# Sketched attention feeding a rational MLP on one core: the same steps in another order, some of them on other engines

## The chip, the cores and the metric

One core of a Trainium2 chip. The metric is the device time of the whole program in microseconds (us), lower is better (a run more than 1.5% above the fastest of its kernel counts as slow). The profile is one execution of the program; its **span** runs from the first to the last instruction and is 1.7 to 1.8 us shorter than the time of that same execution. Engines: PE multiplies matrices, DVE and ACT work on 128 partitions of elements, POOL (GpSimd) here issues DMAs, SP issues loads and stores.

## The reference, cut to what matters

```python
# attention with a polynomial sketch, 4 batches x 4 heads x 1088 tokens x 32
a, b = S1 @ x, S2 @ x                        # 8 features each
phi = outer(a, b)                            # 64 features, for q and for k
kv, z = phi(k)^T v, sum(phi(k))
attn = (phi(q) kv) / (phi(q) z + 1e-6)
# then, on 4352 tokens of 128 channels, with 2048 hidden columns
h = attn @ w_in
P = a0 + a1*h + a2*h*h + a3*h*h*h
Q = 1 + |b0|*|h| + |b1|*h*h
out = (P / (Q + 1e-6)) @ w_out
```

## The kernel before

The kernel is a list of 589 steps. Each step names what it needs and which buffers it takes and gives back. Two constants decide the program: `ENGINE` says on which engine a step runs that may run on several, and `ORDER` says in which order all steps are issued. An engine executes its own steps strictly in that order.

```python
BUFS = dict(xT=3, hb=4, s=2, u=4, t=4, ..., h_ps=3, out_ps=1, w_ps=1, ..., oT=1)
ENGINE = {"k00.ea": "DVE", "k01.ea": "DVE", ..., "g1.ts": "DVE", ..., "g17.us": "DVE", "g18.ts": "DVE", "o8.eT": "DVE"}
ORDER = [27, 4, 26, 30, 0, 36, 1, 31, 6, ...]        # 589 numbers

def issue(self, order):                              # of the plan
    for i in order:
        s = self.steps[i]
        assert all(a["n"] in done for a in s["after"]), s["name"]
        for key in s["take"]:
            self.slot[key] = free[key[0]].pop(0)
        s["fn"]()
        ...
```

Most of the time goes to 20 groups (g0 to g19) of hidden columns, mostly 4096 elements per partition. One group is these steps:

```python
# g.e*  PSUM (where PE leaves its results) -> bf16 copies of h            ACT, or DVE where ENGINE says so
# g.ab  u = |hb|      g.sq  s = hb*hb       DVE
# g.hi  t = a3*hb+a2  g.cu  t = t*s         DVE
# g.lo  hb = a1*hb+a0                       DVE
def add(dst, src, name):                    # g.us: u += s    g.ts: t += hb
    if ENGINE.get(name) == "DVE":
        nc.vector.tensor_add(out=d, in0=d, in1=s)
    else:                                   # an accumulating DMA, issued by GpSimd
        nc.gpsimd.dma_start(out=d, in_=s, accum_op=AX.add, max_dma_last_dim=4096)
# g.ln  L = Ln(u*lsc + 1)   g.ex  u = Exp(-L)        ACT   (1/Q)
# g.ov  t = t*u             DVE    then g.pj: t @ w_out on PE
```

`kBC.*` are steps for keys, `qN.*` for queries, `oN.eT` and `oN.st` the copy and store of an output chunk, `ld.*` loads, `fN` matmuls without use, meant to keep PE's clock up (`SKIP` names those that are left out).

Of the kernel before, what the change touches and what calls it, by code (L numbers as in the profile page):

```python
# [27 lines left out]
ENGINE = {  # L28
    "ld.S0": "ACT", "ld.S1": "ACT", "ld.a": "ACT", "ld.b": "ACT", "k00.ea": "DVE", "k01.ea": "DVE", "kr.ev": "DVE",
    "kr.ea": "DVE", "k0.s0": "DVE", "q1.ev": "DVE", "q2.ev": "DVE", "k20.ea": "DVE", "q5.xe": "DVE", "k30.ea": "DVE",  # L30
    "k31.ea": "DVE", "q7.ev": "DVE", "q8.xe": "DVE", "g1.ts": "DVE", "o0.eT": "DVE", "o1.eT": "DVE", "g7.e4": "DVE",
    "o3.eT": "DVE", "o5.eT": "DVE", "g13.e4": "DVE", "g17.us": "DVE", "g18.ts": "DVE", "o8.eT": "DVE",
}

FOUR = []
SKIP = ["f3"]

HOME = {
    "k00.T": "h_ps", "k00.ab": "h_ps", "k01.T": "h_ps", "k01.ab": "h_ps", "kv.0": "h_ps", "q0.T": "h_ps",
    "q0.xT": "h_ps", "q1.T": "h_ps", "k11.T": "h_ps", "q2.T": "h_ps", "q2.xT": "h_ps", "q3.T": "h_ps",  # L40
    "q3.xT": "h_ps", "k20.T": "h_ps", "k21.T": "h_ps", "kv.2": "h_ps", "q4.T": "h_ps", "q5.T": "h_ps",
    "q6.T": "h_ps", "q8.T": "h_ps", "q8.xT": "h_ps", "fill.1": "h_ps", "fill.4": "h_ps", "fill.6": "h_ps",
    "fill.9": "h_ps", "fill.11": "h_ps", "fill.12": "h_ps",
# [3 lines left out]
    27, 4, 26, 30, 0, 36, 1, 31, 6, 56, 20, 3, 32, 33, 37, 5, 41, 38, 39, 57, 23, 46, 29, 2, 42, 40, 58, 43, 47, 59,  # L47
    60, 44, 45, 48, 49, 50, 51, 52, 21, 53, 28, 55, 8, 61, 7, 83, 78, 79, 67, 54, 62, 63, 80, 81, 11, 34, 68, 69, 12,
    64, 65, 84, 22, 9, 66, 82, 70, 71, 72, 85, 86, 215, 216, 35, 217, 10, 87, 218, 230, 232, 231, 233, 24, 245, 16,
    220, 219, 115, 247, 116, 246, 248, 222, 224, 234, 235, 237, 223, 221, 226, 73, 74, 75, 249, 250, 238, 239, 240,  # L50
    76, 25, 251, 93, 94, 236, 77, 252, 253, 254, 227, 266, 268, 270, 88, 89, 267, 269, 256, 257, 241, 242, 95, 97,
    272, 271, 225, 14, 228, 273, 229, 243, 104, 105, 90, 258, 244, 96, 91, 92, 274, 277, 285, 98, 130, 201, 117, 99,
    100, 255, 260, 286, 13, 275, 131, 279, 259, 287, 101, 278, 289, 291, 261, 262, 288, 118, 119, 276, 200, 290, 292,
    102, 103, 120, 121, 263, 293, 294, 296, 297, 281, 306, 106, 307, 108, 122, 123, 325, 326, 280, 107, 109, 124,
    264, 298, 282, 283, 308, 309, 310, 312, 152, 295, 311, 313, 300, 265, 110, 111, 112, 327, 284, 153, 329, 314,
    315, 331, 328, 317, 318, 319, 330, 132, 332, 205, 125, 126, 301, 113, 213, 154, 334, 18, 114, 299, 155, 134, 302,
    333, 127, 128, 129, 316, 133, 346, 303, 336, 135, 338, 17, 156, 348, 321, 337, 304, 347, 349, 189, 350, 320, 190,
    365, 203, 157, 351, 322, 323, 352, 15, 136, 366, 141, 158, 137, 353, 138, 142, 335, 340, 305, 324, 367, 368, 355,
    354, 139, 339, 357, 358, 359, 369, 140, 386, 159, 341, 371, 370, 372, 342, 160, 376, 373, 374, 377, 378, 387, 19,
    143, 145, 356, 361, 360, 343, 388, 389, 344, 161, 390, 392, 391, 393, 144, 167, 362, 168, 146, 405, 395, 375,  # L60
    406, 162, 163, 164, 165, 345, 380, 381, 166, 363, 409, 147, 397, 394, 148, 149, 364, 398, 399, 407, 411, 408,
    379, 382, 150, 151, 410, 412, 414, 416, 413, 418, 169, 171, 396, 383, 178, 401, 426, 427, 428, 429, 170, 417,
    172, 179, 384, 445, 402, 430, 431, 432, 173, 446, 174, 181, 400, 433, 403, 175, 435, 404, 434, 415, 420, 437,
    180, 182, 176, 447, 177, 448, 419, 451, 421, 183, 438, 439, 449, 422, 450, 452, 454, 453, 385, 466, 467, 209,
    436, 441, 468, 469, 423, 485, 486, 424, 456, 457, 184, 185, 186, 440, 442, 470, 471, 458, 487, 472, 204, 488,
    489, 473, 443, 474, 475, 444, 477, 478, 455, 460, 191, 193, 425, 459, 187, 188, 479, 491, 490, 492, 192, 461,
    493, 194, 462, 506, 525, 526, 508, 507, 476, 494, 480, 195, 196, 463, 527, 496, 497, 464, 481, 509, 482, 498,
    495, 510, 511, 512, 513, 528, 465, 529, 483, 197, 514, 198, 515, 517, 519, 499, 500, 484, 530, 531, 214, 532,
    501, 548, 546, 533, 207, 534, 547, 516, 535, 502, 549, 553, 518, 536, 538, 520, 561, 562, 563, 537, 564, 551,
    550, 552, 521, 522, 523, 574, 540, 503, 504, 575, 576, 554, 577, 539, 555, 541, 208, 542, 566, 524, 579, 581,  # L70
    580, 568, 567, 569, 557, 558, 565, 570, 571, 505, 199, 578, 556, 559, 582, 543, 211, 206, 212, 544, 545, 210,
    560, 572, 573, 583, 584, 585, 586, 587, 588, 202,
# [40 lines left out]
def kernel(  # L113
# [243 lines left out]
    W_by = [big.tile([128, NF // 2, d_model], BF, name=f"w_by{i}") for i in range(4)] if FOUR else []  # L357
    by_steps = []
    if FOUR:
        ld["wf"] = load("wf", lambda key: starter(key).dma_start(  # L360
            out=new("L", "wf")[:, :NF // 2 * d_model].rearrange("p (n d) -> p n d", d=d_model),
            in_=moe_w_out.rearrange("(fo fi) d -> fi fo d", fi=128)[:, 0:NF // 2, :]), 1740, pk=1024, take=[("L", "wf")], start="SP")

        def by(i):
            o, s = W_by[i].rearrange("p n d -> p (n d)"), T["L", "wf"][:, :NF // 2 * d_model]
            if ENGINE.get(f"c.w{i}", "ACT") == "ACT":
                nc.scalar.mul(o, s, a_sb[:, i:i + 1])
            else:
                nc.vector.tensor_scalar(out=o, in0=s, scalar1=a_sb[:, i:i + 1], scalar2=None, op0=AX.mult)

        for i in range(4):
            alts = dict(ACT=280 + 0.82 * NF // 2 * d_model, DVE=150 + 0.55 * NF // 2 * d_model)
            by_steps.append(plan.add(f"c.w{i}", ENGINE.get(f"c.w{i}", "ACT"), alts[ENGINE.get(f"c.w{i}", "ACT")], lambda i=i: by(i),
                                     after=[ld["wf"], c_inv], give=[("L", "wf")], alts=alts))

# [39 lines left out]
    def add_keys(b):  # L415
# [44 lines left out]
        s = plan.add(f"k{b}.rem", "PE", 540, accumulate_rem, after=[prev, krem_step[0], ld["vr"]])  # L460
# [19 lines left out]
    def add_queries(n, srcs, nt, owners, loads, kv_steps, give=()):  # L480
# [41 lines left out]
        def divide():  # L522
            nb = min(2, nt)
            nd = pair("nd")[:, :nt // nb, :nb * 132].rearrange("p b (g c) -> p b g c", c=D + 1)
            den = new("den", n)[:, :nt // nb, :nb * H]
            nc.vector.tensor_scalar(out=den, in0=nd[:, :, :, D], scalar1=1e-6, scalar2=None, op0=AX.add)
            nc.vector.reciprocal(out=den, in_=den)
            x = new("x", n)[:, :nt, :].rearrange("p (b i) (h d) -> p b (i h) d", b=nt // nb, h=H)
            nc.vector.tensor_mul(out=x, in0=nd[:, :, :, 0:D],
                                 in1=den[:, :, :, None].broadcast_to([128, nt // nb, nb * H, D]))  # L530

        def x_transposes():
            p = new(*ps(nm, "xT"))
            for i in range(nt):
                nc.tensor.transpose(p[:, i * 128:(i + 1) * 128], in_=T["x", n][:, i, :], identity=ident)

        def x_evac():
            o, i = new("xT", n)[:, :W], T[ps(nm, "xT")][:, :W]
            if ENGINE.get(nm + ".xe", "ACT") == "ACT":
                nc.scalar.mul(o, i, sig)  # L540
            else:
                nc.vector.tensor_scalar(out=o, in0=i, scalar1=sig, scalar2=None, op0=AX.mult)
# [3 lines left out]
        ex = [plan.add(f"{nm}.ex{i}", "PE", 900 * W // 512 + 80, lambda i=i: expand(i), after=[s, c_rep],  # L546
# [5 lines left out]
        for i in range(nt // 2):  # L552
            nd.append(plan.add(f"{nm}.nd{i}", "PE", 520, lambda i=i: num_den(i), after=[s] + nd + kv_steps,
                               take=[("h_ps", nm, "nd")] if i == 0 else [], give=[("q_pT", n)]))
        s = plan.add(f"{nm}.dv", "DVE", 560 + 135 * nt, divide, after=nd, take=[("x", n), ("den", n)],
                     give=[("h_ps", nm, "nd"), ("den", n)])
        s = plan.add(nm + ".xt", "PE", 100 * nt + 37, x_transposes, after=[s], take=[ps(nm, "xT")], flex=[ps(nm, "xT")], give=[("x", n)])
        return add_copy(nm + ".xe", x_evac, W, ptr=1, after=[s, c_b], take=[("xT", n)], give=[ps(nm, "xT")])


# [224 lines left out]
```

## Time and profile before

| | before |
|---|---|
| time, median of the first 3 runs | 251.48 us (251.42 to 254.35, and that last one counts as slow) |
| profiled execution | 250.56 us, span 248.8 |
| DVE busy / ACT busy | 225.4 / 213.7 us |
| DMA: queue 0, that is the accumulating sums and w_out | 79.7% of the span |

Busy time is time in which at least one instruction of the engine runs. How these lines are read, and those of the waits and timelines, stands in the prediction, which shows them.

The timelines of DVE and POOL before (start, duration in us) have:

```profile
28.11 1.79 DVE L585 TENSOR_SCALAR u<-hb 128x2048 int16<-128x2048 int16 x1
...
26.83 1.34 POOL L594 DMA_DIRECT2D u<-s  x1 [23.34 <-DVE u L585]
27.51 1.88 POOL L265 DMA_DIRECT2D w_out<-in_moe_w_out_dram  x1
```

The same mask takes 0.69 us elsewhere. Here it runs while GpSimd issues two DMAs one upon the other.

### The profile page before, as it was taken

The numbers are of one execution on the slowest core, as the hardware profiler recorded it, in microseconds if no ns is written. First come the engines' busy times: TensorE is split into PE (matmuls) and PEld (weight loads), VectorE is DVE, ScalarE is ACT, GpSimd is POOL, SyncE is SP. The second block draws the span as 40 slices with busy tenths as digits, with TensorE's granted clock in tenths as the row PEclk, the third lists the DMA queues.
The fourth block names the chain that finished last, engine by engine and source line by source line (L and its number), as shares of the span: only waits on it lengthen the run. The fifth ranks groups of instructions, "written<-read, shape, count | busy, mean of one in ns | idle before, by whom it ended". The sixth has DMA issues, their size and how long they took to land.

```text
span 248.8 us, 4279 instructions
## 1 busy us (share of the span) xinstructions
PE 222.5 (89%) x1789; PEld 127.1 (51%) x1789; DVE 225.4 (91%) x205; ACT 213.7 (86%) x158; POOL 48.8 (20%) x61
## 2 busy tenths in 40 slices
PE   7999999999999999998999899999998969920763
PEld 2674455654636465553657354546453627720532
DVE  0785999998989989998999999999999999998993
ACT  3335589989989798989999999899999899899990
POOL 4000422132101212121111221122031312113210
PEclk9999999999999999999999999999999999995599
DMA  5994498999998899979999999999999999999982
GB/s 149 315 278 172 72 147 173 174 219 185 176 169 182 147 192 223 232 166 173 169 177 202 171 171 171 211 169 171 189 172 186 182 201 187 179 184 186 200 162 68
DMA packets 23427, 45.11 MB, mean 181 GB/s; under 512 B 5232, under 2 KB 13552, under 8 KB 23408
## 3 DMA queue, kind: packets, MB, share of 16 engines
q0 software_dynamic: 11232, 34.87, 79.7%
q1 hardware_dynamic: 11712, 9.90, 12.6%
q8 instruction: 14, 0.23, 0.4%
q10 hardware_dynamic: 464, 0.08, 0.2%
q14 instruction: 5, 0.04, 0.0%
HBM read 8.79 MB, written 2.23 MB: 44 GB/s over the span
## 4 chain that ended last, share of the span: by engine, by line
DVE 31%; PE 31%; DMA 20%; ACT 10%; issue 8%; SPq 0%; DVEq 0%; ACTq 0%; POOLq 0%
PE h_ps L572 15%; DMA u<-s 12%; DVE t L621 7%; DVE s L582 6%; DMA t<-hb 5%; DVE t L607 4%; DVE u L585 4%; PE h_ps L499 4%; ACT u L618 4%; DVE t L603 3%; PE out_ps L629 3%; ACT L L614 3%; DVE hb L610 2%; ACT hb L184 2%; DMA q<-in_q_dram 2%
## 5 line engine op out<-in xcount | busy, mean ns | idle before, releaser
L572 PE MATMUL h_ps<-xT,w_in_sb 128*128 128x512 f32 (+1 forms) x288 | 126.0, 577 | 4.2 <-ACT hb L184 2.7
L572 PEld LDWEIGHTS h_ps<-xT,w_in_sb 128*128 128x128 f32 x288 | 51.7, 190 | 56.5 <-issue 43.1
L184 ACT CAST hb<-h_ps 128x1024 bf16<-128x1024 f32 x66 | 64.8, 1020 | 8.2 <-PE h_ps L572 7.8
L614 ACT ACTIVATE L<-u,one_ap,lsc 128x4096 f32<-128x4096 bf16 (+2 forms) x20 | 65.9, 3295 | 6.4 <-DMA u<-s 6.3
L618 ACT ACTIVATE u<-L 128x4096 bf16<-128x4096 f32 (+2 forms) x20 | 62.3, 3116 | 0.2
L629 PE MATMUL out_ps<-w_out,t 128*128 128x128 bf16 x544 | 35.2, 225 | 15.8 <-DVE t L621 15.7
L594 POOL DMA_DIRECT2D u<-s x19 | 24.1, 1269 | 118.9 <-DVE u L585 54.5
L629 PEld LDWEIGHTS <-t 128*128 128x128 bf16 x544 | 32.5, 101 | 23.8 <-DVE t L621 20.6
L621 DVE TENSOR_TENSOR t<-t,u 128x4096 bf16<-128x4096 bf16 (+2 forms) x20 | 39.2, 1968 | 4.0 <-ACT u L618 2.2
L582 DVE TENSOR_TENSOR s<-hb 128x4096 bf16<-128x4096 bf16 (+2 forms) x20 | 39.2, 1963 | 1.5 <-ACT hb L184 1.5
L607 DVE TENSOR_TENSOR t<-t,s 128x4096 bf16<-128x4096 bf16 (+2 forms) x20 | 39.3, 1967 | 0.3
L594 POOL DMA_DIRECT2D t<-hb x18 | 21.6, 1200 | 72.2 <-issue 20.1
L610 DVE TENSOR_SCALAR hb<-hb,a_sb 128x4096 bf16<-128x4096 bf16 (+2 forms) x20 | 23.8, 1189 | 0.2
L603 DVE TENSOR_SCALAR t<-hb,a_sb 128x4096 bf16<-128x4096 bf16 (+2 forms) x20 | 23.6, 1183 | 0.0
L585 DVE TENSOR_SCALAR u<-hb 128x4096 int16<-128x4096 int16 (+2 forms) x20 | 22.3, 1115 | 0.1
L499 PE MATMUL h_ps<-qT,Srep 64*128 64x512 f32 (+1 forms) x72 | 19.5, 617 | 0.4 <-ACT hb L184 0.4
L506 DVE TENSOR_TENSOR q_pT<-A_sb,h_ps 128x1024 f32<-128x1024 f32 (+1 forms) x9 | 10.4, 1157 | 2.6 <-ACT A_sb L184 1.4
L519 PEld LDWEIGHTS h_ps<-kv,q_pT 128*64 128x64 f32 (+1 forms) x288 | 8.7, 134 | 5.1 <-issue 2.0
L519 PE MATMUL h_ps<-kv,q_pT 128*64 128x66 f32 (+1 forms) x288 | 10.1, 224 | 0.0
L184 ACT COPY A_sb<-h_ps 128x1024 f32<-128x1024 f32 (+1 forms) x9 | 8.7, 965 | 0.8 <-PE h_ps L499 0.8
L499 PEld LDWEIGHTS h_ps<-qT,Srep 64*128 64x128 f32 x72 | 5.4, 184 | 6.9 <-ACT hb L184 2.1
L184 ACT COPY kT<-h_ps 128x512 f32<-128x512 f32 x5 | 2.9, 585 | 5.3 <-PE h_ps L383 4.8
(89 smaller groups left out, 137.0 us busy)
## 6 DMA issues: line engine op xcount, KB each, us to landing
u<-s POOLq DMA_DIRECT2D x15, 1024.0 KB, 8.6
t<-hb POOLq DMA_DIRECT2D x15, 1024.0 KB, 9.5
k_sb<-in_k_dram SPq DMA_DIRECT2D x4, 512.0 KB, 4.3
q<-in_q_dram SPq DMA_DIRECT2D x8, 256.0 KB, 4.9
v<-in_v_dram SPq DMA_DIRECT2D x4, 512.0 KB, 8.2
out_dram<-oT SPq DMA_DIRECT2D x8, 256.0 KB, 7.0
w_in_sb<-in_moe_w_in_dram SPq DMA_DIRECT2D x2, 512.0 KB, 4.8
u<-s POOLq DMA_DIRECT2D x2, 512.0 KB, 7.7
```

What stands on the lines that cost most here:

```text
L184: nc.scalar.copy(out=out, in_=in_)
L499: nc.tensor.matmul(pair(i)[:, g, :W], lhsT=Srep[i][rows].rearrange("p g f -> p (g f)"), rhs=T["qT", n][rows, :W], start=True, stop=True)
L572: nc.tensor.matmul(p[:, i * W:(i + 1) * W], lhsT=w_in_sb[:, fi * 128:(fi + 1) * 128], rhs=T["xT", n][:, :W], start=True, stop=True)
L582: nc.vector.tensor_mul(out=new("s", g)[:, :gw], in0=h, in1=h)
L585: nc.vector.tensor_scalar(out=new("u", g)[:, :gw].bitcast(mybir.dt.int16), in0=T["hb", g][:, :gw].bitcast(mybir.dt.int16), scalar1=0x7FFF, ...
L594: nc.gpsimd.dma_start(out=d, in_=s, accum_op=AX.add, max_dma_last_dim=4096)
L603: nc.vector.tensor_scalar(out=new("t", g)[:, :gw], in0=T["hb", g][:, :gw], scalar1=a_sb[:, 3:4], scalar2=a_sb[:, 2:3], op0=AX.mult, op1=AX ...
L607: nc.vector.tensor_mul(out=T["t", g][:, :gw], in0=T["t", g][:, :gw], in1=T["s", g][:, :gw])
L614: nc.scalar.activation(out=new("L", g, l0)[:, :lw], in_=T["u", g][:, l0:l0 + lw], func=ACT.Ln, bias=one_ap, scale=lsc)
L618: nc.scalar.activation(out=T["u", g][:, l0:l0 + lw], in_=T["L", g, l0][:, :lw], func=ACT.Exp, scale=-1.0)
L621: nc.vector.tensor_mul(out=T["t", g][:, :gw], in0=T["t", g][:, :gw], in1=T["u", g][:, :gw])
L629: nc.tensor.matmul(T["out_ps", n][:, j * 128:(j + 1) * 128], lhsT=T["t", g][:, c:c + 128], rhs=W_out[:, fis[i], :], start=fis[i] == 0 and ...
```

## The change

The order and the engines were searched anew with a schedule model in which consecutive instructions of ACT and of DVE overlap. Code for variants that were not in use (`FOUR`) is taken out and another is put in (`SPLIT`, an empty list); neither runs. What runs differently is this, cut:

```diff
 ENGINE = {
-    ..., "k00.ea": "DVE", "k01.ea": "DVE", "kr.ev": "DVE", "kr.ea": "DVE", "k0.s0": "DVE", "q1.ev": "DVE", "q2.ev": "DVE",
-    "k20.ea": "DVE", "q5.xe": "DVE", "k30.ea": "DVE", "k31.ea": "DVE", "q7.ev": "DVE", "q8.xe": "DVE", "g1.ts": "DVE",
-    "o0.eT": "DVE", "o1.eT": "DVE", "g7.e4": "DVE", "o3.eT": "DVE", "o5.eT": "DVE", "g13.e4": "DVE", "g17.us": "DVE",
-    "g18.ts": "DVE", "o8.eT": "DVE",
+    ..., "k00.ea": "DVE", "kr.ea": "DVE", "k0.s0": "DVE", "k0.s1": "DVE", "q0.A": "DVE", "q1.A": "DVE", "k10.ev": "DVE",
+    "k21.ea": "DVE", "g0.us": "DVE", "g1.us": "DVE", "g5.e6": "DVE", "g6.us": "DVE", "o4.eT": "DVE", "g11.e2": "DVE",
+    "g15.e6": "DVE", "g15.ts": "DVE", "g18.ts": "DVE", "g19.e0": "DVE", "g19.us": "DVE", "o8.eT": "DVE",
 }
-SKIP = ["f3"]
+SKIP = ["f13", "f4"]
 ORDER = [
-    27, 4, 26, 30, 0, 36, 1, 31, 6, 56, 20, 3, 32, 33, 37, 5, 41, 38, 39, 57, 23, 46, 29, 2, 42, 40, 58, 43, 47, 59,
+    4, 27, 26, 30, 0, 36, 1, 28, 6, 31, 32, 33, 37, 56, 41, 57, 38, 39, 20, 46, 29, 58, 42, 43, 40, 47, 60, 44, 10,
     ... (all 589 in another order; HOME, which says in which PSUM pool small tiles live, likewise)
```

## The prediction

> **What bounds the kernel now.** I read the page from the top: busy shares, slices, then the waits of each engine, the chain, and the table by windows of 10 us. The parts of the page that carry the reading:
>
> ```profile
> span 248.8 us, 4279 instructions
> PE 222.5 (89%) x1789; PEld 127.1 (51%) x1789; DVE 225.4 (91%) x205; ACT 213.7 (86%) x158; POOL 48.8 (20%) x61
> DVE  0785999998989989998999999999999999998993
> DMA  5994498999998899979999999999999999999982
> q0 software_dynamic: 11232, 34.87, 79.7%
> ```
>
> Three resources are near full at once. DVE is busy 225.4 of 248.8 us, ACT 213.7, and the DMA row stands at 9 nearly everywhere from the sixth slice on. PE's 89% is modelled and says less. Next, where DVE stands idle. Three windows of that table (columns: window, length, then PE, PEld, DVE, ACT, POOL busy with instruction counts, PE clock, DMA share, GB/s):
>
> ```profile
> 0.00:10.00 10.00, 8.24 (x61) 4.35 (x63) 3.15 (x10) 3.89 (x5) 2.69 (x23) 1.00 0.67 205
> 140.00:150.00 10.00, 9.15 (x58) 4.80 (x57) 9.96 (x8) 9.57 (x8) 2.59 (x2) 1.00 0.96 172
> 240.00:248.80 8.80, 3.34 (x37) 2.08 (x35) 4.09 (x6) 3.05 (x4) 0.79 (x1) 1.00 0.35 82
> ```
>
> Over all windows DVE idles 10.9 us in 0 to 30 us, 7.8 us in the 210 us from 30 to 240, and 4.7 us after that: 23.4 in all, which with 225.4 is the span. In the body DVE is 96% busy, so DVE is the bound, with ACT close behind and DMA full. The waits of DVE, ACT and POOL show what it and its neighbours wait for:
>
> ```profile
> DVE t L621 <- ACT u L618: 2.2, 4, 0.7
> DVE t L621 <- DMA t<-hb: 1.8, 4, 0.7
> ACT hb L184 <- PE h_ps L572: 7.8, 12, 1.6
> ACT L L614 <- DMA u<-s: 6.3, 8, 1.2
> ```
>
> No DVE wait in the body is long. The full DMA shows as 6.3 us of ACT waiting for u<-s and 1.8 us of DVE waiting for t<-hb, no more. The chain does list DMA with 20%, but a share of a chain is not what its removal would give, for the engines do other work meanwhile.
>
> Last, how instructions follow each other. From the timelines of DVE and of ACT:
>
> ```profile
> 38.75 2.29 DVE L582 TENSOR_TENSOR s<-hb 128x4096 bf16<-128x4096 bf16 x1
> 40.95 1.34 DVE L603 TENSOR_SCALAR t<-hb,a_sb 128x4096 bf16<-128x4096 bf16 x1
> 42.33 2.29 DVE L607 TENSOR_TENSOR t<-t,s 128x4096 bf16<-128x4096 bf16 x1
> ...
> 63.55 3.82 ACT L614 ACTIVATE L<-u,one_ap,lsc 128x4096 f32<-128x4096 bf16 x1
> 67.26 1.01 ACT L184 CAST hb<-h_ps 128x1024 bf16<-128x1024 f32 x1
> ```
>
> The square ends at 41.04, yet the next, independent instruction starts at 40.95: an overlap of 0.09 us. That one ends at 42.29, and the cube, which reads its result, starts at 42.33: a gap of 0.04. So a DVE instruction right behind the one that it needs costs some 0.12 us more than behind another. On ACT the overlap is 0.11 us, and an Exp right behind its own Ln starts 0.03 late (217.76 plus 3.80 against 221.59): 0.14.
>
> **What the Trainium skill says.** "ScalarE: Activation LUTs", section "What ACT_TABLE_LOAD costs", has back-to-back ACTIVATEs overlap by about 93 ns; the trace agrees within 20 ns, for independent ones only. "Perfetto Trace Analysis", section "Optimizing Scalar/DVE Operations", explains why for both engines: the write-acknowledgement half of the overhead overlaps with the next instruction. "VectorE: DVE Perf Modes", section "The perf-mode tier table", gives 1224 ns for a bf16 tensor_tensor of 2048 elements; L592's two adds of that size took 1224 and 1226 ns. "SBUF — State Buffer", section "Who interferes with whom", says that a 2-port DVE instruction and GpSimd block each other. The trace may hold one case: the 2048-wide bit mask of L585 at 28.11 us took 1.79 us instead of 0.69, beside two DMA issues of POOL. It is one in 205, so I give it 1 us either way.
>
> **The change, part by part.** The arithmetic is untouched. The deleted FOUR branches were empty and SPLIT is empty, so nothing of either runs. What changes is which engine takes a step, and the order.
>
> *Sums u+=s and t+=hb between the DMA queue and DVE.* On DVE newly: g0.us and g1.us (2048 wide, 1.22 each), g6.us and g15.ts (4096, 2.29 each, taken from L607, the same operation and shape), g19.us (1024, 0.69): 7.7 us. Off DVE: g1.ts and g17.us, 1.22 each: 2.4. DVE +5.3 us. The DMA loses 13 and gains 4 units of 1024 columns. It now moves 131 such units (66 for u<-s, 65 for t<-hb) in 79.7% of 248.8 = 198 us, with the one w_out load in it, so at most 1.51 us each. Net 9 units: about 13.5 us less DMA work, 93% to 87% of the present span.
>
> *PSUM copies between ACT and DVE.* Off DVE: k01.ea, kr.ev, q1.ev, q2.ev, q7.ev, three more small ea, q5.xe, q8.xe, four oT copies, g7.e4 and g13.e4. With 0.69 for a 512-wide copy, 1.22 for a 1024-wide one, 0.29 for a small one, 0.43 for kr.ev, 0.75 and 0.48 for the two xe: 10.0 us. On DVE newly: k0.s1 0.22, q0.A and q1.A 1.22 each, k10.ev 0.69, k21.ea 0.29, one oT 0.68, and four 1024-wide evacuations (g5.e6, g11.e2, g15.e6, g19.e0) at 1.22: 9.2. DVE −0.9. On ACT the same steps give +8.9 and −7.8 (0.60, 1.02, 0.28 a copy): +1.1 us.
>
> *Order.* I decoded the two lists into step names by engine and counted the neighbours where the second step needs the first. On DVE 22 become 8, on ACT 7 become 4: 14 × 0.12 = 1.7 us back on DVE, of which 1.2 is more overlap and 0.5 less gap, and 0.4 us on ACT. Three fewer DVE instructions lose three overlaps, 0.3 us.
>
> *Sum for DVE.* 225.4 + 5.3 − 0.9 − 1.2 + 0.3 = **228.9 us busy**: the bound itself goes up by 3.5. ACT goes to about 214.5. A gain can come only out of the 23.4 us that DVE idles.
> - Start, 0 to 30 us. ACT waits there in short steps for PE (four of 0.7 to 1.6 us), and DVE waits 1.41 for A_sb and 1.46 for hb from ACT. With q0.A and q1.A on DVE the first kind goes; g0.us on DVE spares the first Ln a trip through DMA (it waited 0.64 us). PE still sets when the first h is there. I take 9.5 instead of 10.9.
> - Body. Shorter DMA queues and fewer dependent neighbours should halve the 7.8: 4.
> - End. The last transfer t<-hb was issued at 239.93 and landed 3.7 us later; now g19.us is on DVE, so one transfer fewer stands ahead of it. After the last Exp the rest stays: product, projection, copy, store. I take 4.5 instead of 4.7.
>
> Sum 18.0, span 246.9. The median of the runs lies 2.7 us above the profiled span before (251.48 against 248.8); with that, **249.6 us**, 0.7% faster.
>
> **The rivals.**
> 1. *DMA is the real bound.* It is full, 13.5 us of it go, and u<-s takes 8.6 us from issue to landing though one transfer needs about 6. For: the DMA row, and the chain's 20%. Against: engines' waits on it sum to 8.1 us. If it were so, the span would fall by up to those waits while DVE stayed level: 244, 246 to 247 us, hardly over 2%. DVE's 228.9 plus the start (9) and the end (4.4) and 2 for small gaps make 244.3, which is about the floor.
> 2. *DVE merely gets longer.* If idle time does not shrink, because it comes from PE and ACT order and not from DMA, the span is 228.9 + 23.4 = 252.3, so 255 us. Against: the steps moved were chosen to fit a schedule with the true overlaps.
> 3. *A new wait in a new order.* The first half of w_in goes out behind q2, v0, v_rem, k1 and q1 instead of fifth; before, it was issued at 5.94 and its first reader began at 19.9, while DMA is full from 10 to 20 us. Now it starts at about 9.5; with 4.8 us to landing it has some 5 us in hand. If it misses, all is late by that much, 1 to 3 us.
> 4. *ACT becomes the bound.* It gets 1 us more and already waits 7.8 us for PE. That eats gains, 1 to 2 us.
>
> **Range and chances.** Floor 247, centre 249.6, nothing gained 255. An 80% range of 246.6 to 253.0. Faster by over 2% needs under 246.45, below the floor: 0.09. Slower by over 2% needs over 256.5, so all idle time kept and a new wait besides: 0.04. Within 2%: 0.87.
>
> **What would show it.** In the profile of the changed kernel: DVE busy 228 to 230, ACT 214 to 215; queue 0 at 184 to 186 us of the span; 16 u<-s transfers (now 19) and 18 t<-hb (as now); DVE idle in 30 to 240 us at 3 to 5; ACT waits for u<-s under 4 us; the first projection's matmul at 19 to 20.5 us; the issue-to-landing median of u<-s below 8. I am wrong if DVE busy comes out lower than now (overlaps larger than counted, or shorter instructions), if body idle stays at 8 or more, or if the first h matmul comes after 21 us because w_in is late.

## The result

The changed kernel takes **245.31 us** (244.75 to 245.44, 4 runs) against 251.45 us (250.43 to 254.35, 4 runs, one of them slow) of the kernel before. Ratio 0.9765, 95% interval 0.973 to 0.9799: faster by 2.35%. Ratios here are the mean time of one kernel's fast runs over that of the other's of the same rounds, so not quite the ratio of the medians.

The page of the changed kernel, its span, busy times, two rows of slices and the DMA queue:

```profile
span 243.7 us, 4275 instructions
PE 222.8 (91%) x1787; PEld 129.3 (53%) x1787; DVE 227.2 (93%) x203; ACT 213.6 (88%) x163; POOL 44.7 (18%) x58
DVE  0888989999999999999999999999999999999991
DMA  5996089989999996899979999999999999899870
q0 software_dynamic: 10544, 32.51, 75.8%
```

DVE is busy longer than before, 227.2 against 225.4, in a span that is 5.1 us shorter. Windows at the same places (columns as in the prediction), and the waits:

```profile
0.00:10.00 10.00, 8.57 (x70) 4.64 (x72) 3.58 (x10) 3.09 (x5) 2.68 (x23) 1.00 0.69 194
140.00:150.00 10.00, 10.00 (x64) 4.90 (x62) 9.68 (x11) 10.00 (x7) 1.73 (x2) 1.00 1.03 188
240.00:243.70 3.70, 0.00 (x0) 0.00 (x0) 0.42 (x1) 0.00 (x0) 0.00 (x0) 0.67 0.14 35
```

```profile
DVE t L626 <- ACT u L623: 1.4, 2, 1.3
ACT hb L184 <- PE h_ps L577: 6.4, 9, 1.9
ACT L L619 <- DMA u<-s: 1.6, 3, 0.8
```

ACT's wait for u<-s is down from 6.3 to 1.6 us, and DVE no longer waits for t<-hb at all. Which of these is cause and which is company, the page can't say.

How steps follow each other now, in the timeline of DVE:

```profile
37.70 2.29 DVE L587 TENSOR_TENSOR s<-hb 128x4096 bf16<-128x4096 bf16 x1
39.91 1.22 DVE L590 TENSOR_SCALAR u<-hb 128x4096 int16<-128x4096 int16 x1
41.05 1.34 DVE L608 TENSOR_SCALAR t<-hb,a_sb 128x4096 bf16<-128x4096 bf16 x1
42.30 1.22 DVE L626 TENSOR_TENSOR t<-t,u 128x2048 bf16<-128x2048 bf16 x1
43.44 2.28 DVE L612 TENSOR_TENSOR t<-t,s 128x4096 bf16<-128x4096 bf16 x1
```

Another group's last product (L626) stands between the linear step and the cube that reads it, and every instruction starts 0.08 to 0.09 us before the one ahead ends. Adding up all of DVE's instructions in the two traces (durations, minus overlaps, plus gaps):

| DVE, us | before | after | difference |
|---|---|---|---|
| sum of the durations | 236.0 | 239.5 | +3.4 |
| overlaps (pairs that touch or overlap) | −10.6 (128) | −12.3 (149) | −1.6 |
| gaps up to 0.1 us | 1.8 (52) | 1.2 (37) | −0.6 |
| longer gaps | 17.5 (24) | 11.1 (16) | −6.3 |
| before its first and after its last instruction | 4.1 | 4.1 | 0.0 |
| span | 248.8 | 243.7 | −5.1 |

And along the way: the first h matmul starts at 19.90 before and 20.16 after (+0.3 us); from there to the end of group 12's last product it takes 173.9 and 170.8 us (−3.1); from there to the end 55.0 and 52.7 us (−2.4). So the gain is made in the body and at the end, nothing of it in the head. Between 30 us and the last 12 us the longer gaps of DVE went from 6.6 to 1.5 us. Before, 3.3 us of them ended with PE, 2.2 with ACT and 1.1 with a transfer t<-hb; now 0.8 with PE, 0.7 with ACT and none with a transfer.

### The profile page after: what moved, and what is told of

The parts are those of the page before. It is cut to its first block, busy times and chain, and to the rows that moved or that the text cites. A ratio compares the mean times of both kernels' runs of the same rounds, so it can differ in the third digit from the quotient of the medians.

```text
span 243.7 us, 4275 instructions
## 1 busy us (share of the span) xinstructions
PE 222.8 (91%) x1787; PEld 129.3 (53%) x1787; DVE 227.2 (93%) x203; ACT 213.6 (88%) x163; POOL 44.7 (18%) x58
## 3 DMA queue, kind: packets, MB, share of 16 engines
q0 software_dynamic: 10544, 32.51, 75.8%
## 4 chain that ended last, share of the span: by engine, by line
PE 41%; DVE 36%; DMA 10%; issue 9%; ACT 2%; DVEq 0%; ACTq 0%; POOLq 0%
PE h_ps L577 21%; DVE t L626 8%; DVE s L587 7%; DVE t L612 5%; PE out_ps L634 5%; DVE u L590 4%; DMA t<-hb 4%; DVE hb L615 4%; DMA u<-s 4%; PE h_ps L480 4%; DVE t L608 4%; PE w_ps L402 2%; PE h_ps L500 2%; DMA k_sb<-in_k_dram 2%; PE h_ps L402 1%
## 5 line engine op out<-in xcount | busy, mean ns | idle before, releaser
L634 PE MATMUL out_ps<-w_out,t 128*128 128x128 bf16 x544 | 36.6, 229 | 13.5 <-ACT oT L184 7.5
L634 PEld LDWEIGHTS <-t 128*128 128x128 bf16 x544 | 33.7, 103 | 21.9 <-DVE t L626 19.2
L599 POOL DMA_DIRECT2D t<-hb x18 | 21.0, 1165 | 112.4 <-DVE hb L615 37.4
L626 DVE TENSOR_TENSOR t<-t,u 128x4096 bf16<-128x4096 bf16 (+2 forms) x20 | 39.3, 1965 | 1.6 <-ACT u L623 1.4
L599 POOL DMA_DIRECT2D u<-s x16 | 19.9, 1242 | 76.6 <-DVE u L590 38.4
L590 DVE TENSOR_SCALAR u<-hb 128x4096 int16<-128x4096 int16 (+2 forms) x20 | 21.1, 1060 | 0.5 <-ACT hb L184 0.5
L487 DVE TENSOR_TENSOR q_pT<-A_sb,h_ps 128x1024 f32<-128x1024 f32 (+1 forms) x9 | 10.4, 1154 | 0.0
L500 PE MATMUL h_ps<-kv,q_pT 128*64 128x66 f32 (+1 forms) x288 | 10.4, 225 | 0.0
L184 ACT COPY A_sb<-h_ps 128x1024 f32<-128x1024 f32 (+1 forms) x7 | 6.8, 968 | 0.1
L402 PEld LDWEIGHTS w_ps<-v,k_p 128*64 128x64 f32 x192 | 5.9, 138 | 1.8 <-issue 0.9
```

The lines of the kernel that those rows point to most:

```text
L184: nc.scalar.copy(out=out, in_=in_)
L626: nc.vector.tensor_mul(out=T["t", g][:, :gw], in0=T["t", g][:, :gw], in1=T["u", g][:, :gw])
L634: nc.tensor.matmul(T["out_ps", n][:, j * 128:(j + 1) * 128], lhsT=T["t", g][:, c:c + 128], rhs=W_out[:, fis[i], :], start=fis[i] == 0 and ...
```

## The experiments

Three theories. **A**: the new order made the gain. **B**: the sums moved to DVE relieved the full DMA, and that made it. **C**: order and engines are one thing, fitted to each other. Names starting with a are versions of the changed kernel, with b of the kernel before. Of the 16 runs, 14 computed the correct result and two were wrong on purpose. They were taken in other rounds than the changed kernel's 245.31 us; differences from it in us can be off by half a microsecond.

### Order and engines apart

```diff
 # a_eng_before: ORDER, HOME of the changed kernel
-ENGINE = {... as changed ...}
+ENGINE = {... as before ...}
 # b_eng_after: ORDER, HOME of the kernel before
-ENGINE = {... as before ...}
+ENGINE = {... as changed ...}
```

> The changed kernel's order of steps and PSUM homes, but every step on the engine that it had before (all 23 entries of the old engine table, none of the new). DVE busy should fall by about 3.5 us and the DMA queue gets its 9 units of 1024 columns back. Theory A, the gain is the order's: about 245 to 247 us, most of the gain stays. Theory B, the gain is that the DMA was relieved by sums moved to DVE: 249 to 252 us, the gain is gone, with ACT's wait for u<-s back at 5 us or more. Theory C, order and engines belong together and neither works alone: over 252 us.

> The old order of steps and PSUM homes, with every step on the engine that it has in the changed kernel. Theory A, order: 251 to 255 us, no gain or a loss by the 3.5 us of DVE work. Theory B, relief of the DMA: 246 to 248 us. Theory C, neither alone: over 254 us.

Measured: 274.4 us (ratio to before 1.091, interval 1.085 to 1.097) and 278.7 us (1.101, 1.094 to 1.109). Each half of the change alone costs 9 or 10%; together they gain 2.35%. That is theory C, and more drastic than expected. HOME and SKIP went with the order in both runs; neither was tried by itself. DVE's busy time stayed what loads say, 224.0 and 229.5 us; the longer gaps rose from 11 and 17 us to 41 and 42.

Smaller parts go the same way:

```diff
 # b_sums_after: the kernel before
-"g1.ts": "DVE", "g17.us": "DVE",
+"g0.us": "DVE", "g1.us": "DVE", "g6.us": "DVE", "g15.ts": "DVE", "g19.us": "DVE",
 # b_g6us: the kernel before, only
+"g6.us": "DVE",
 # a_copies_before: the changed kernel with the sums as changed and all other entries of ENGINE as before
```

> The kernel before, its order and copies, with all the sums where the changed kernel has them (DVE +5.3 us, DMA 13.5 us less). If sums are what helps whatever the order: under 250 us. If they only add to the bound in the old order: 255 us or more.

> The kernel before with only the 4096-wide sum g6.us moved from the DMA queue to DVE (2.3 us of DVE work). If the local trouble of that transfer (12.4 us in the chain) made the loss that the change took away there: 248.5 to 250 us. If the old order can't use it: 251.5 to 254 us.

> The changed kernel, its order and sums, with the PSUM copies back on the engines that they had before (DVE +0.9 us, ACT 1.1 us less). By load alone: 245 to 247 us. If the order was fitted to these copies: 255 us or more, with single waits of several us.

Measured: 268.3 us (1.066, interval 1.062 to 1.071), 256.6 us (1.021, 1.017 to 1.026) and 259.2 us (1.033, 1.028 to 1.037). My guess for b_g6us, that one badly placed transfer was the loss, is refuted. Its timelines of DVE and ACT show how 2.3 us of work came to cost 5.4:

```profile
106.35 0.17 DVE L527 TENSOR_SCALAR den<-h_ps 128x16 f32<-128x16 f32 x1 [0.67 <-PE h_ps L520]
...
107.45 2.28 DVE L593 TENSOR_TENSOR u<-u,s 128x4096 bf16<-128x4096 bf16 x1
...
109.83 3.81 ACT L615 ACTIVATE L<-u,one_ap,lsc 128x4096 f32<-128x4096 bf16 x1 [3.52 <-DVE u L593]
```

In the old order the sum's place lies behind a division that itself waits for PE. As a transfer it did not stand in DVE's line; as a DVE instruction it does, and the Ln waits 3.52 us for it; before, it waited 1.23 us for the transfer. PE then stands idle, and what follows is a second cost that busy times don't show. PE's timeline of b_g6us:

```profile
110.24 1.88 PE L573 MATMUL h_ps<-xT,w_in_sb 128*128 128x512 f32 x4
...
115.17 2.74 PE L573 MATMUL h_ps<-xT,w_in_sb 128*128 128x512 f32 x4 [3.05 <-ACT xT L541]
```

From 116.3 to 119.7 us the trace records the granted clock at 0.50. Such stretches between the first and the last h matmul add up to 6.8 us in b_g6us, 10.2 in b_sums_after, 10.4 in a_eng_before and 13.7 in b_eng_after. In the profiles of the kernel before and of the changed kernel there is none. In these four runs each began 3 to 5 us after the start of a PE gap of some 2 us or longer; not every such gap was followed by one (2.26 us in the kernel before and 3.05 us in b_sums_after were not). At full clock h matmuls start every 0.43 us, inside a stretch every 0.83 to 0.93 us (medians). An estimate from this is that PE loses about half of a stretch's length, 3 to 7 us in these runs, which is at most a part of what they lose. So a gap that a misfit opens can be paid twice.

In a_copies_before, the order had ACT issue the load of b after a copy that now ran there:

```profile
14.40 0.35 ACTq L242 DMA_DIRECT2D b_sb<-in_moe_b_dram  x1
...
18.98 0.17 DVE L343 TENSOR_SCALAR b_abs<-b_sb 128x2 int32<-128x2 int32 x1 [4.73 <-DMA b_sb<-in_moe_b_dram]
```

That puts the first h matmul at 25.50 instead of 20.16 us, 5.3 of its 13.9 us. So a good part of what a_copies_before loses is such an accident of the head, which a new search of the order might mend; none was made. These runs show that neither half can be had alone as it stands; they don't give the worth of either.

### Is it the DMA?

The cleanest test here takes work off the DMA and touches no engine.

```diff
 # b_half_sums and a_half_sums: wrong results on purpose
+if dst == "t" and g in (4, 7, 9, 11, 13):
+    d, s = T[dst, g][:, :gw // 2], T[src, g][:, :gw // 2]
 nc.gpsimd.dma_start(out=d, in_=s, accum_op=AX.add, max_dma_last_dim=4096)
```

> The kernel before, its order and engines untouched, with five of the transfers t<-hb (groups 4, 7, 9, 11, 13) cut to half their columns: wrong results on purpose. The DMA loses 10 units of 1024 columns, about 15 us of its work, as the change takes from it, and no engine gains or loses an instruction. Theory B, relief of the DMA alone makes the gain: 245 to 247 us. Theory C, the old order can't use it: 249.5 us or more.

> The changed kernel with the same five transfers cut to half (wrong results on purpose): another 15 us less DMA work. If the DMA still costs the changed kernel anything, 242 to 244 us; if its remaining idle time is PE's and ACT's order alone (ACT waits only 1.6 us for u<-s), 244.5 us or more.

Measured: 252.8 us (1.007, interval 1.003 to 1.012) and 245.0 us (0.977, 0.973 to 0.981). The queue and span of the two:

```profile
span 252.8 us, 4275 instructions
q0 software_dynamic: 10592, 32.25, 72.6%
```

```profile
span 243.4 us, 4272 instructions
q0 software_dynamic: 9904, 29.89, 69.9%
```

The kernel before, relieved by as much DMA work as the change takes, gets no faster: the fastest of its six runs took 251.7 us. The changed kernel, relieved once more, is where it was (0.977 and 0.9765). So less DMA work does not by itself make the gain, and theory B in that form is refuted. One form of it is left untested. The change took u<-s transfers away, and this probe cut t<-hb: ACT still waited 4.8 us for u<-s (6.3 before), and DVE 3.1 us for t<-hb (1.8 before). Relief of just those transfers that the engines waited for, without more work on DVE, was not tried. The Trainium skill, "Perfetto Trace Analysis", section "Identifying the Most-Contended Engine", warns that occupancy of the 16 DMA engines misleads. In the old order it did: a DMA row of nines, and 15 us less of it gained nothing.

The old kernel's half sums even cost 0.7%. Its profile is the slowest of the six runs (254.59 us), and PE ran at half pace in it twice. In the first transposes (1.09 us for four, 0.63 before) the first record of a full clock comes at 10.0 us, against 4.3 before, and the first h matmul came at 21.99 us. At the end a set of h matmuls took 3.52 us where before it took 1.98; there the granted clock is 0.50 from 204.5 to 207.9 us. Why the clock was low then is open. Between the two, from the first h matmul to group 12, it took 173.0 us, 0.9 less than before. That can't be credited to the relief, for b_wo_later below, with the same DMA work as before, took 172.9 us there.

Putting DMA work on is another matter.

```diff
 # a_dma_probe: store each of chunks 2 to 7 four times
+for _ in range(1 if 2 * b + c < 2 else 4):
     nc.sync.dma_start(out=out[...], in_=oT)
 # a_dma_loads: behind those stores, three loads that nobody reads
+for i in range(3):
+    nc.sync.dma_start(out=idle_sb[:, i % 2], in_=moe_w_in[:, i * 512:(i + 1) * 512])
```

> The changed kernel with each of the six later full output stores (chunks 2 to 7) issued four times instead of once, the same bytes to the same place: 18 extra stores of 256 KB, 4.5 MB, by the 3.2 us per MB of the hardware queue before about 14 us of DMA work, as much as the change took from the DMA, and no work on any engine. Theory B, the DMA relief made the gain: 248 to 251 us. Theory A: within 1 us of 245.3.

> The changed kernel with three more plain loads of 256 KB into an unread tile behind each of the last six full stores: 18 loads, 4.5 MB, some 14 us of DMA work, and this time no buffer that an engine uses is held longer (in the run with repeated stores the copies into oT waited 13.6 us for them). Theory B, the DMA relief made the gain: 248 us or more, with ACT's and DVE's waits on u<-s and t<-hb up by several us. Theory A, the order removed idle time that had little to do with DMA: 245 to 246.5 us.

The first gave 258.3 us (1.027) and tells nothing of the DMA: the one oT buffer was held until the fourth store, as its waits show, so the probe made its own wait.

```profile
ACT oT L184 <- DMA out_dram<-oT: 9.1, 3, 4.1
DVE oT L186 <- DMA out_dram<-oT: 4.5, 1, 4.5
```

The second gave 250.5 us (0.9996, interval 0.996 to 1.003): 14 us of DMA work put back cost 5.2 us, and ACT waited 6.1 us for u<-s. 1.0 us of the 5.2 lies behind DVE's last instruction, at the stores. By my own criterion the run speaks for theory B. With the half sums beside it, it says that the changed kernel has little room on the DMA: work added in the way costs nearly the whole gain, work removed gains none. The relief may thus be needed for the gain; it is not enough for it.

One more try at the coupling gave the two widest sums back to the queue:

```diff
 # a_two_sums_pool
-"g6.us": "DVE", "g15.ts": "DVE",
```

> The changed kernel with the two 4096-wide sums g6.us and g15.ts given back to the DMA queue, all else as it is: DVE busy down by 4.4 us, DMA up by 12 us. Theory B, DMA relief: slower, 248 to 252 us. DVE alone bounds: faster, 241 to 243 us. Theory C, the order fits these engines only: slower, with one or two new waits of 2 to 6 us for exactly these transfers.

Its six runs fell into 253.7 us once and 257.6 to 259.1 five times, and those five count as slow beside the one. So there is no ratio and the profiled run is not used; even the fastest run is 8 us slower than the changed kernel, with 4 us less work on DVE.

### Which engine has room?

```diff
 # a_dve_probe: the square of groups 4, 8, 11, 14 twice
+if g in (4, 8, 11, 14):
+    nc.vector.tensor_mul(out=T["s", g][:, :gw], in0=h, in1=h)
 # a_act_probe: the Exp of groups 4 and 11 twice
+for _ in range(2 if g in (4, 11) else 1):
     nc.scalar.activation(..., func=ACT.Exp, scale=-1.0)
```

> The changed kernel with the square of four groups (4, 8, 11, 14) computed twice: 4 x 2.20 us = 8.8 us more on DVE, the same result. If DVE bounds the whole of the body: 254 us. If the changed kernel has slack on DVE: under 250 us.

> The changed kernel with the Exp of groups 4 and 11 computed twice: 2 x 3.5 us = 7.0 us more on ACT, nothing more on DVE. If ACT bounds as well: 251 to 252 us. If only DVE bounds and ACT has slack (it idles some 4 us in the body): 246 to 249 us.

Measured: 255.2 us (1.016, interval 1.011 to 1.021) and 255.8 us (1.019, 1.015 to 1.023). By the traces DVE's busy time rose by 9.5 us (the squares take 2.29 us, not 2.20), and that cost 9.9; ACT's rose by 7.4, and that cost 10.4. Neither has room. That ACT's work cost more than itself doesn't make ACT the tighter of the two: in its probe the granted clock was at 0.50 for 10.2 us in two stretches behind the doubled Exps, where PE had stood idle 3.25 and 3.15 us (6.8 us in the probe of DVE), and a set of h matmuls took 3.78 us instead of 1.98. The prediction's "DVE is the bound, with ACT close behind" is better said: both are on the path by turns.

### What neighbours that need each other cost

```diff
 # a_adjacent: in ORDER of the changed kernel, g.hi moved to right ahead of its reader
-..., g9.sq, g9.hi, k31.pd, g9.cu, ...
+..., g9.sq, k31.pd, g9.hi, g9.cu, ...        (11 groups)
```

> The changed kernel with 11 of DVE's linear steps (t = a3 h + a2) moved later, to stand right ahead of the cube or the second linear step that needs them: 11 more neighbours that depend on each other, nothing else. At 0.12 us each, 1.3 us more of DVE time, all on the bound: 246.6 us if DVE sets the end throughout. If slack absorbs them: under 245.7 us.

Measured: 248.1 us (0.986, interval 0.982 to 0.990), 2.7 us slower than the changed kernel by the medians, 2.3 by the two ratios. In its trace the overlaps shrink by 0.81 us and the short gaps grow by 0.31: 1.1 us for 11 pairs, 0.10 each, against the 0.12 read off the trace before. Another 1.3 us is longer gaps, above all one wait of 1.65 us for ACT. So the cost per pair came close to the forecast, it is paid in full, and in this trace the late steps went with other waits as well.

### The stalled mask

```diff
 # b_wo_later: POOL's order in the kernel before
-g0.us, ld.wo, g1.us, g0.ts, ...
+g0.us, g1.us, ld.wo, g0.ts, ...
```

> The kernel before with the w_out load issued behind g1.us instead of right behind g0.us[...]. If the mask of 1.79 us (0.69 elsewhere) was stalled by it, that mask goes to 0.69 and DVE busy falls by 1.1 us; on the time 250.3 us if it lay on the path, within 0.4 us of the kernel before if not.

Measured: 250.8 us (0.9992, interval 0.995 to 1.004). The three masks of that width, grouped by form:

```profile
L586 DVE TENSOR_SCALAR u<-hb 128x2048 int16<-128x2048 int16 x3 | 2.1, 685 | 0.0
```

They were 3.2 us with a mean of 1052 ns before. The stall is gone, DVE busy fell by 0.9 us to 224.5, and the time did not follow: the 1.1 us lay where DVE had slack.

### A better version?

```diff
 # a_head_tail: ACT's order; and group 1 as sq, hi, ab, cu, lo
+ld.S1, ld.b, k00.ev, ...
-..., g18.ln0, o7.eT, g18.ex0, g19.ln0, ...
+..., g18.ln0, g18.ex0, o7.eT, g19.ln0, ...
 # a_tail: only the move of g18.ex0
```

> A try at a better version: the changed kernel with three small moves. The load of b goes out second instead of behind kT's copies (DVE waited 0.3 to 1.5 us for it); g18.ex0 goes ahead of the copy o7.eT (ACT waited 0.82 us for PE there, and the last product 1.29 us for ACT); group 1's five DVE steps reordered so that none follows the one that it needs. 0.3 + 0.9 + 0.1: 244 us, correct result.

> The changed kernel with one move: g18.ex0 ahead of the copy o7.eT on ACT. In the run with three moves this alone cut DVE's last wait for ACT from 1.29 to 0.45 us, while the early load of b made v late by 1.1 us. So 244.4 us, correct; if the end is set by something else: 245.3.

Measured: 245.4 us (0.978, interval 0.974 to 0.981) and 245.2 us (0.976, 0.973 to 0.980): both equal to the changed kernel. DVE's last wait for ACT did fall from 1.29 to 0.45 us in both. In a_head_tail the head took it back; its timelines of SP and of PE:

```profile
1.78 3.35 SPq L229 DMA_DIRECT2D k_rem<-in_k_dram  x4
...
10.96 1.15 PE L403 MATMUL h_ps<-v,k_p 128*64 128x64 f32 x32 [0.94 <-DMA v<-in_v_dram]
```

With b's load issued at 1.73 us, four small loads take SP 3.35 us instead of 1.96, v goes out 0.6 us later, and PE waits. This holds in all 18 traces: 3.3 to 3.7 us in the seven with b early, 1.95 to 1.98 in the eleven others. In a_tail the first h matmul came 0.4 us later than in the changed kernel's profile by chance, and the rest took 223.0 us against 223.5. A gain of half a microsecond is inside the noise of the runs, so no version that beats both kernels is claimed.

## Why the prediction was wrong

It forecast 249.6 us, 0.7% faster, in a range from 246.6; it is 245.31, 2.35% faster. The mechanism was the right one in outline: DVE gets more work, and the gain comes out of its idle time. The sum was off by 4.2 us against the profiled execution (245.44 us), in three terms.

- **The work on DVE**, forecast 228.9 us, measured 227.2: 1.7 us. 1.0 us of it is the sum of durations (+3.4 instead of +4.4), since the mask that stalled 1.1 us before ran unhindered. I had seen that and given it 1 us either way; it could only go down. 0.7 us is overlap: 21 more overlapping pairs came, not 11. 15 came out of short gaps, as counted (14), and 8 out of longer gaps that closed, which the sum had left out; there are 2 pairs fewer in all.
- **The idle time**, forecast 18.0 us, measured 16.5: 1.5 us. Start 8.9 (forecast 9.5; DVE's wait for A_sb went as said, but ACT's waits for PE ahead of the first copies of h did not, 3.8 us before and 4.9 after). Body 2.3 (forecast 4; the part up to the last 12 us, with its short gaps; 30 to 240 us, as the prediction had it, is 4.4, but that now takes in most of the end). End 5.3 (forecast 4.5). The body is the step that failed in kind: "should halve" had nothing behind it, and 6.6 us of longer gaps became 1.5. What closed them, the order or the shorter waits for transfers, the runs don't separate.
- **From span to time**, forecast 2.7 us, measured 1.7: 1.0 us. I subtracted the span of one execution from the median of others. The profiled execution before had taken 250.56 us, 1.8 more than its own span. The floor of 247 us was too high by this and by the first term, and with it the chance of 0.09 for faster by over 2%.

The other steps. ACT's busy time was forecast at 214 to 215 and is 213.6. The queue was forecast at 184 to 186 us and is 75.8% of 243.7, or 184.7. The counts of transfers (16 and 18), ACT's wait for u<-s (1.6, under 4) and the first h matmul (20.16, between 19 and 20.5) came as said. The landing of u<-s did not: 8.7 us, not under 8 (that of t<-hb went from 9.5 to 8.5). One count was off by one: an Exp stands right behind its own Ln 6 times in the kernel before, not 7, and 4 times now.

Of the rivals, the first (DMA is the real bound) came closest in number, 246 to 247 us. As the sole reason it is refuted: as much less DMA work without the new order gained nothing. But most of the wait for u<-s went away with the change (6.3 to 1.6 us), the half sums did not take it away (4.8), and DMA work put back took most of the gain. So relief as a part of the reason stays possible. The second (DVE merely gets longer) is what b_sums_after and b_eng_after show, and worse. The third (w_in late) did not come. The fourth (ACT becomes the bound) did not come as told, since ACT's busy time did not grow; but ACT has no room.

What stays open: how much order and how much assignment each give, and how much of the order's gain is shorter waiting for u<-s. A search of the order for each assignment could tell more.

## What to carry to other kernels

When engines run their steps in a fixed order and several of them are over 85% busy, an assignment is worth something only with an order made for it: price moved steps by the gaps that they open, not by their durations alone, and look at the granted clock behind each gap of PE. Test a full DMA by taking work off it before blaming it: here 15 us less in the old order were worth nothing. Take it off the transfers that somebody waits for. And put an independent instruction between two that need each other; each such pair cost 0.10 us on DVE.

## What the Trainium skill lacked or had wrong

- "VectorE: DVE Perf Modes", section "The DRAIN you can't avoid", says that a next op which is not held starts before the pipe is empty; it lacks by how much, and what an op right behind the one that it needs costs. Here independent DVE instructions mostly start 0.08 to 0.09 us before the one ahead ends (149 pairs touch or overlap in the changed kernel), one that needs it starts some 0.04 us after, and 11 such pairs forced on the kernel cost 1.1 us.
- "ScalarE: Activation LUTs", section "What ACT_TABLE_LOAD costs", has the overlap of 93 ns; here 0.11 us. It lacks that an Exp right behind its own Ln starts 0.03 us late instead.
- "SBUF — State Buffer", section "Who interferes with whom", has the mutual blocking of 2-port DVE instructions and GpSimd, but not how long a DVE instruction waits beside DMA issues. Here a 2048-wide mask took 1.79 us instead of 0.69 beside two issues at once, and 0.69 when they were parted.
- No page that I read has what an accumulating DMA between two SBUF tiles costs: at most 1.51 us of all 16 engines per 1024 bf16 columns on 128 partitions (131 of these in 198 us, a w_out load included).
- No page that I read has how much a small load issued from ACT lengthens SP's own issues beside it: four loads took SP 3.3 to 3.7 us where ACT had issued b's load at 1.7 us, and 1.95 to 1.98 where it issued it later.
